# A local attention tile summed by identity products on TensorE, part of the approximate exponentials' additions moved to GpSimd, and the gate products split

## The chip, the cores and the metric

The kernel runs on one core of a Trainium2 chip. The time is the device time of one execution in microseconds (us). The engines are named as in the profile: PE (TensorE matmuls; PEld its weight loads), DVE (VectorE), ACT (ScalarE), POOL (GpSimd), SP (SyncE, which here issues nearly all DMAs). The five run their own instruction streams in order and wait for each other through semaphores.

## The reference

Input x is 2048 rows of 512, bf16. Two attention blocks A and B read the same x, each with its own weights, 32 heads of 16 columns, and their outputs are mixed row by row with a gate:

```python
g = sigmoid((x * gate_w).sum(-1, keepdims=True))
a = A_ref(x, A_wqkv, A_wo)    # full softmax attention: every row sees all 2048 rows
b = B_ref(x, B_wqkv, B_wo)    # local: row s sees rows s, s-2, ..., s-14 (8 of them), masked below row 0
return g * a + (1 - g) * b
```

In B, for one row and head: `logits[w] = q . k[s - 2w] / 4`, a softmax over the 8 values, and `o = sum over w of attn[w] * v[s - 2w]`.

## The kernel before

**Block A** has 32 periods: four blocks of 512 query rows by eight groups of four heads (`periods`). In a period there are 16 tiles of 128 key rows, with four heads each: 64 score blocks of 128 keys by 512 queries, 2048 in all. Each is one matmul of PE with 32 rows of weights; four heads lie in the four row groups of the array and can run side by side. A score block is turned into exponentials in one of two ways:

- Exactly, on ACT: PE writes three or two blocks into one of two PSUM rings (`ring`), ACT reads them with one activation and writes `pT` in bf16 (`act_source`), and PE multiplies `pT` with the values and the ones column of `vp_all` into the period's accumulator `acc` (`emit_pva`).
- Approximately, on DVE, by whole tiles of four blocks, called quads (`make_quad`): PE writes a block into a PSUM bank `m`, DVE multiplies and adds so that the result, written as uint16, is read as the bf16 bit pattern of the exponential (`conv`, four of 128x512). Two further terms are the same numbers plus 42 and plus 85 (`OFFS`); each is one DVE addition over the whole 128x2048 quad (`term`). PE multiplies the three terms with the values and with two weighted copies of them, `vd_all`, and adds them up in `acc` (`emit_pvd`). A quad can only come from the last four key tiles of a period.

At the end of a period DVE transposes `acc`, takes the reciprocal of the sums, POOL scales, and DVE transposes back (`post`). There is one accumulator; the next period's sums wait until it is read.

**Block B** has 16 tiles of 128 rows (`b_tile`). PE projects K, V and Q of the tile, DVE copies them out of PSUM, SP stores K and V into a DRAM scratch `kv_scr` and loads them back eight times, shifted by two rows each (`ksh`, `vsh`, 128 x 8 x 512 bf16). POOL then does nearly everything: eight products q * k, a tree of additions over the 16 columns of a head, the softmax with short steps on DVE and ACT between, eight products of attention and value into f32 tiles (`amul`), seven additions over the eight (`aadd`, `fin1`), the last with a bf16 output `obb`. PE transposes `obb` in 16 small pieces (`fin2`), and DVE copies the result as `obt` (`fin3`). `padd` chains a tile's POOL steps one after the other, but other POOL work can stand between them.

**The gate** is 64 matmuls of one column each (`zmm`), an exponential on ACT and three short DVE operations. **The output** (`final`) multiplies, for each of 16 row tiles, four chunks of `obt` with B's output weights and four of A's result with A's into one PSUM bank; DVE multiplies with the gate, SP stores. For the last four tiles all parts but one of A's are done early and kept in f32; the last part, and the addition, follow the last period.

**The order of the work** is written by a planner inside the kernel (`Sched`), which runs when the program is built. It holds a list of operations with estimated durations, dependencies, buffers (`Hold`, `Slots`) and due times, and takes, over and over, the operation that can begin soonest on its engine, among near ones the one that is due first. The engines' instruction streams come out in that order. What bears on the change:

- `MARGIN` adds a pause to a dependency between two engines, so that an operation is placed only so long after its input's estimated end.
- `warm` and `zero_pass` put matmuls of zeros (`zw` with `ones_t`) into PE's stream. The planner adds up what PE streamed in the last 3413 ns (`share`; a matmul on a quarter of the array counts a quarter). Under `STREAM` a zero matmul may go in where it delays nothing much; under `LEAST` it goes in even with a small delay.
- `lock=True` marks DVE operations that the planner keeps from overlapping with a POOL operation.
- `start_quad` starts a quad on DVE whenever DVE is estimated to be done with it before ACT would have reached that tile, and no other PE work is overdue. So the number of blocks that DVE takes over follows from the planner's estimates of all engines.
- `hooks` runs when a period begins and adds the projections, the gate (period 0) and the B tiles that then come due.
- The loads at the start are issued by SP in the order of their due times, with a time at which the planner expects each to land.

Every instruction passes through one helper (`chain_on`, called at line 382), so that all instructions have line 382 in the profile; they are told apart by the names of their tiles.

Of the kernel before, what the change touches and what calls it, by code (L numbers as in the profile page):

```python
# [10 lines left out]
ALU = mybir.AluOpType  # L11
AX = mybir.AxisListType
FP32 = mybir.dt.float32
BF16 = mybir.dt.bfloat16
# [5 lines left out]
DH = 16  # L20
# [34 lines left out]
PASS = 216.0  # L55
SWITCH = 100.0

MARGIN = {("POOL", "DVE"): 1500.0, ("POOL", "PE"): 1500.0, ("DVE", "PE"): 200.0, ("PE", "DVE"): 60.0,
          ("ACT", "DVE"): 1000.0, ("DVE", "POOL"): 800.0, ("SP", "POOL"): 1500.0, ("POOL", "ACT"): 1000.0}
WINDOW = 3413.0  # L60
STREAM = 0.48
LEAST = 0.42
FAST = 682.0


# [52 lines left out]
class Sched:  # L118
# [31 lines left out]
    def pe_run(self, mms, start, state=None, count=False):  # L150
        t, mode, busy = (self.t["PE"], self.pe_mode, list(self.pe_busy)) if state is None else state
        busy = list(busy)
        t = max(t, start)
        first = None
        last = t
        for m, tile_, cols in mms:
            if m != mode:
                if state is None and count:
                    self.switches += 1
                t = max(t, max(busy) + (SWITCH if "r" in (m, mode) else 0.0))  # L160
                mode = m
            ks = range(4) if tile_ is None else (tile_,)
            t = max(t, max(busy[k] for k in ks))
            if first is None:
                first = t
            if count:
                self.streamed.append((t, t + cols / 2.4, 1.0 if tile_ is None else 0.25))
            for k in ks:
                busy[k] = t + cols / 2.4 + 2.5
            last = t + 174.0 + cols / 2.4  # L170
            t += 15.0
        return first, last, (t, mode, busy)
# [159 lines left out]
def kernel(  # L332
# [138 lines left out]
    def dma(o, i):  # L471
        return lambda: SP.dma_start(out=o, in_=i)
# [34 lines left out]
        ld[(kind, 0)] = S_.add(Op("SP", lambda: None, dur=1.0, due=-9.0, lat=7000.0, name=f"ld_{kind}"))  # L507
    load("x0", x_load(0), 8100.0)
    load("x1", x_load(1), 11500.0)
    load("wv", dma(wv[:, :, G1:D], a_w3[:, :, 2 * D + G1:3 * D]), 9000.0)  # L510

    def gw_load():
        with nc.allow_non_contiguous_dma(reason="tiny gate vector load"):
            SP.dma_start(out=gw[:], in_=gate_w.rearrange("(c p) -> p c", p=128))
    load("gw", gw_load, 9000.0)
    load("bw", dma(bw[:], B_wqkv.rearrange("(c p) n -> p c n", p=128)), 12000.0)

    def pad_load():
        for k in range(2 * D // 128):
            SP.dma_start(out=kv_scr[0:16, 128 * k:128 * k + 128], in_=zw[0:16, :])  # L520
    ld["pad"] = S_.add(Op("SP", pad_load, dur=4500.0, due=2000.0, lat=3000.0, name="ld_pad"))
# [177 lines left out]
    def g_jobs(due):  # L699
        st = {}  # L700
        hz = Hold("m")

        def zmm():
            st["zp"] = misc_ps(hz, [128, NT])
            for t in range(NT):
                for c in range(DC):
                    mm(st["zp"][:, t:t + 1], xT[:, c, t * 128:(t + 1) * 128], gw[:, c:c + 1], c == 0, c == DC - 1)

        def zexp():
            st["e1"] = const.tile([128, NT], FP32, name="e1")  # L710
            A.activation(out=st["e1"][:], in_=st["zp"][:], func=ACT.Exp, scale=-1.0)

        def zfin():
            d1 = const.tile([128, NT], FP32, name="d1")
            V.tensor_scalar_min(out=ratio[:], in0=st["e1"][:], scalar1=1.0e30)
            V.tensor_scalar_add(out=d1[:], in0=ratio[:], scalar1=1.0)
            V.reciprocal(out=gate[:], in_=d1[:])
        ops = [Op("PE", zmm, mms=[("f", None, 70)] * 64, due=due, deps=[o for v in xt_ops.values() for o in v] + [ld["gw"]],
                  acq=[hz], not_before=due - 4000.0, name="z"),
               Op("ACT", zexp, dur=250.0, allow=0.0, rel=[hz], name="zexp"),  # L720
               Op("DVE", zfin, dur=600.0, allow=3000.0, name="zfin")]
        S_.chain(ops)
        g_done.append(ops[-1])
# [14 lines left out]
    def b_tile(t, due):  # L738
# [71 lines left out]
            if t == NT - 1:  # L810
                S_.add(lv)
        pool = []
        hp = [Hold("prod") for _ in range(3)]

        def padd(fn, dur, after_last=True, early=False, **kw):
            late = len(pool) > 17 and not early
# [75 lines left out]
        hobb = Hold("osb")  # L892

        def amul(w_, k):
            def s():
                if w_ == 0:
                    st["prod"] = work.tile([128, WH, D], FP32, name="prod", tag="prod", bufs=1)
# [6 lines left out]
        def aadd(k):  # L904

            def s():
                prod = st["prod"]
                G.tensor_tensor(out=prod[:, k, :], in0=prod[:, k, :], in1=prod[:, k + 1, :], op=ALU.add)
            return s

        def fin1():
            obb = sb(hobb, [128, D], BF16, "obb")
            G.tensor_tensor(out=obb[:], in0=st["prod"][:, 0, :], in1=st["prod"][:, 1, :], op=ALU.add)
            st["obb"] = obb
        level, added = [], False
        for w_ in range(W):
            padd(amul(w_, len(level)), 1094.0, after_last=added or w_ == 0, acq=[hp[2]] if w_ == 0 else [], deps=[lv] if w_ == 0 else [],
                 rel=[hvs, hlg] if w_ == W - 1 else [])
            level.append(0)
            added = False  # L920
            while len(level) > 1 and level[-1] == level[-2] and len(level) + level[-1] < 5 and (level[-1] < 2):
                padd(aadd(len(level) - 2), 1268.0)
                added = True
                level.pop()
                level[-1] += 1
        padd(fin1, 1270.0, acq=[hobb], rel=[hp[2]])
        hb = Hold("m")
        obt_hold[t] = Hold("keep")

        def fin2():  # L930
            st["ptp"] = misc_ps(hb, [128, DC, 128], BF16)
            for c in range(DC):
                for c4 in range(4):
# [7 lines left out]
        f = [Op("PE", fin2, mms=[("c", j, 128) for _ in range(DC) for j in range(4)], allow=4000.0, acq=[hb, obt_hold[t]], rel=[hobb],  # L941
                deps=[pool[-1]], name="bf2"),
             Op("DVE", fin3, dur=415.0, allow=800.0, rel=[hb], name="bf3")]
        S_.chain(f)
        obt_ops[t] = f[-1]

# [363 lines left out]
    LATE = 2000.0  # L1310
    QUAD = 6000.0
    UNIT = 470.0
    quad_at = [0]
    quad_end = [None]

# [37 lines left out]
    def make_quad(p, t, late):  # L1353
        i = periods[p][1]
        hq = [Hold("dt") for _ in OFFS]
        q = dict(p=p, t=t, hold=hq, terms=[], late=late)

        def term_tile():
            q["terms"].append(sb(hq[len(q["terms"])], [128, 4, QW], U16, "dt"))
        aops, fops = [], []  # L1360
        for j in range(4):
            hold = Hold("m")
# [9 lines left out]

            def conv(j=j, st=st):
                if j == 0:
                    term_tile()
                V.tensor_scalar(out=q["terms"][0][:, j, :], in0=st["s"][:], scalar1=EXP_MULT, scalar2=EXP_ADD,
                                op0=ALU.mult, op1=ALU.add)
            f_ = S_.add(Op("PE", fill, mms=[("r", j, 512)], deps=[qt_ops[periods[p]][0], kdep(p, t)],
# [5 lines left out]
                           name="conv"))  # L1384
            aops.append(a_)
        tops = []
        for k in range(1, len(OFFS)):
            def term(k=k):
                term_tile()
                V.tensor_scalar(out=q["terms"][k][:], in0=q["terms"][0][:], scalar1=float(OFFS[k]), scalar2=None, op0=ALU.add)  # L1390
            tops.append(S_.add(Op("DVE", term, dur=FAST, lock=True, deps=aops + tops[-1:], acq=[hq[k]], due=min(S_.now + 7000.0 + 1500.0 * k, late - 4000.0 + 1000.0 * k), name="term")))

        def done(o):
            d_busy[0] -= 1
            q["vis"] = o.vis
            pvd_ready.append(q)
        tops[-1].after = done
        d_busy[0] += 1

    def d_source(e):  # L1400
# [31 lines left out]
    def hooks(p):  # L1432
# [90 lines left out]
```

## Time and profile before

| | us |
|---|---|
| median of 3 runs | 819.74 (811.35 to 826.09) |
| the profiled execution | 810.39 |
| its span, first to last instruction | 808.5 |
| ACT busy | 753.4 |
| PE busy | 734.4 |
| POOL busy | 705.7 |
| DVE busy | 691.1 |
| score exponentials on ACT, 650 | 745.2 |
| DVE conversions (128x512), 424 | 277.2 |
| DVE additions (128x2048), 212 | 235.6 |
| mean granted PE clock | 0.971 |

The profile page gives for each engine the busy time, its share of the span and the number of instructions, then the span in 40 slices with tenths of busy time (the row PEclk is the clock granted to PE, in tenths of full speed), then the chain of work that ended last, followed back from the last instruction. Groups of instructions carry tile names, output first: `dt<-m_ps` is a DVE conversion of a score block, `dt<-dt` a DVE addition for a further term, `prod<-vsh,lg` a POOL product of values and attention. A group's busy time counts overlapping instructions once, so it can be less than count times mean. Busy times of PE are of pipelined matmuls with modelled ends; a PE that is 91% busy is not at its peak. A line of the waits reads: engine and tile that waited, what it waited for, us in total, times, longest.

### The profile page before, as it was taken

What the parts mean: (1) busy time and instruction counts of PE and PEld (TensorE: products, weight loads), DVE (VectorE), ACT (ScalarE), POOL (GpSimd) and SP (SyncE); (2) the same over time, 40 slices, a digit from 0 to 9 for tenths busy, and PEclk for the clock granted to TensorE, in tenths of its full rate; (3) what the DMA queues carried; (4) which work ended last, traced back from release to release, by engine and by line L of the source; (5) the groups of instructions that cost most, each with busy time, mean ns of one, the idle gap of its engine ahead of it and who ended that gap; (6) DMA issues with size and microseconds to landing.
All of it is one profiled execution on the core that took longest, in us unless ns stands there. A gap on an engine that the chain in (4) does not pass through costs nothing.

```text
span 808.5 us, 19646 instructions
## 1 busy us (share of the span) xinstructions
PE 734.4 (91%) x8132; PEld 232.4 (29%) x8183; DVE 691.1 (85%) x1019; ACT 753.4 (93%) x680; POOL 705.7 (87%) x615
## 2 busy tenths in 40 slices
PE   7989989899989898999999989999989999999896
PEld 2332222232322213222332222233222222223222
DVE  3635889989999898999999899999988998888974
ACT  3998889998999979998999999999999999999993
POOL 1289798999999979897998999999897999999995
PEclk9997999999999979998999999999989999999998
DMA  8470210220115211011215211111013110212101
GB/s 202 141 117 1 67 53 28 91 67 30 42 50 78 68 53 60 20 54 53 67 51 42 67 53 66 54 49 60 26 53 92 53 54 17 66 64 67 60 14 34
DMA packets 100937, 48.22 MB, mean 60 GB/s; under 512 B 61936, under 2 KB 98288, under 8 KB 100848
## 3 DMA queue, kind: packets, MB, share of 16 engines
q1 hardware_dynamic: 99264, 46.57, 21.3%
q8 instruction: 64, 1.05, 0.5%
q10 hardware_dynamic: 1584, 0.39, 0.2%
q14 instruction: 25, 0.20, 0.1%
HBM read 38.54 MB, written 6.32 MB: 55 GB/s over the span
## 4 chain that ended last, share of the span: by engine, by line
DVE 32%; PE 28%; ACT 27%; issue 9%; SPq 2%; DMA 1%; ACTq 0%; DVEq 0%
ACT pT L382 27%; DVE dt L382 23%; PE m_ps L382 13%; PE acc L382 8%; PE ring L382 7%; DVE kt_all L382 2%; DVE qt L382 2%; SPq L382 2%; DMA bw<-in_B_wqkv_dram 1%; DVE kmax_all L382 1%; DVE kvs L382 1%; DVE accT L382 1%; DVE qb L382 0%; DVE kadd L382 0%; DVE oat L382 0%
## 5 line engine op out<-in xcount | busy, mean ns | idle before, releaser
L382 ACT ACTIVATE pT<-ring 128x1536 bf16<-128x1536 f32 (+2 forms) x650 | 745.2, 1292 | 29.9 <-PE ring L382 28.1
L382 PE MATMUL ring<-qt,kt_all 32*128 32x512 bf16 x1624 | 280.4, 389 | 30.6 <-ACT pT L382 24.9
L382 DVE TENSOR_SCALAR dt<-m_ps 128x512 uint16<-128x512 f32 x424 | 277.2, 676 | 30.5 <-PE m_ps L382 19.4
L382 POOL TENSOR_TENSOR prod<-prod 128x512 f32<-128x512 f32 x224 | 291.8, 1308 | 10.4
L382 DVE TENSOR_SCALAR dt<-dt 128x2048 uint16<-128x2048 uint16 x212 | 235.6, 1114 | 1.1 <-PE acc L382 0.6
L382 POOL TENSOR_TENSOR prod<-ksh,qb 128x512 f32<-128x512 bf16 x128 | 164.8, 1315 | 37.7 <-DVE kt_all L382 33.0
L382 PEld LDWEIGHTS <-kt_all 32*128 32x128 bf16 (+1 forms) x2304 | 94.2, 92 | 299.8 <-issue 284.4
L382 PE MATMUL m_ps<-qt,kt_all 32*128 32x512 bf16 x424 | 149.5, 390 | 19.7 <-DVE dt L382 13.5
L382 PE MATMUL acc<-pT,vp_all 128*17 128x512 bf16 x1624 | 158.9, 389 | 3.4 <-issue 3.0
L382 POOL TENSOR_TENSOR prod<-vsh,lg 128x512 f32<-128x512 bf16 x128 | 156.1, 1239 | 2.9
L382 PEld LDWEIGHTS <-vp_all 128*17 128x17 bf16 x2048 | 46.1, 88 | 112.0 <-issue 102.7
L382 PE MATMUL acc<-dt,vd_all 128*17 128x512 bf16 x848 | 65.8, 386 | 0.8 <-DVE dt L382 0.8
L382 PE MATMUL m_ps<-bw,xT 128*32 128x512 bf16 x768 | 56.7, 395 | 2.1 <-DVE dt L382 0.8
L382 PE MATMUL acc<-ones_t,zw 128*32 128x512 bf16 (+1 forms) x230 | 50.0, 400 | 3.2 <-DVE accT L382 2.0
L382 PE MATMUL acc<-dt,vp_all 128*17 128x512 bf16 x424 | 42.3, 389 | 0.8 <-issue 0.8
L382 PEld LDWEIGHTS <-xT 128*32 128x32 bf16 (+1 forms) x1152 | 32.3, 97 | 33.7 <-issue 26.5
L382 PE MATMUL m_ps<-xT,wkd 128*32 128x512 bf16 x512 | 39.9, 406 | 2.2 <-DMA xT<-in_A_x_dram 0.9
L382 POOL TENSOR_TENSOR ott<-accT,rden 128x256 bf16<-128x256 f32 x31 | 22.9, 740 | 21.5 <-DVE rden L382 20.0
L382 PE MATMUL m_ps<-xT,wqd 128*32 128x512 bf16 x496 | 35.8, 382 | 0.6 <-DVE kt_all L382 0.3
L382 PEld LDWEIGHTS <-zw 128*128 128x128 bf16 (+1 forms) x285 | 17.3, 95 | 53.1 <-issue 51.3
L382 DVE CAST kvs<-m_ps 128x512 bf16<-128x512 f32 x32 | 21.7, 680 | 12.4 <-PE m_ps L382 12.3
L382 DVE CAST qt<-m_ps 128x512 bf16<-128x512 f32 x31 | 21.1, 680 | 12.1 <-PE m_ps L382 11.9
(69 smaller groups left out, 409.2 us busy)
## 6 DMA issues: line engine op xcount, KB each, us to landing
ksh<-kv_scr SPq DMA_DIRECT2D x16, 1024.0 KB, 5.4
vsh<-kv_scr SPq DMA_DIRECT2D x16, 1024.0 KB, 5.5
kv_scr<-kvs SPq DMA_DIRECT2D x16, 256.0 KB, 2.0
out_dram<-osb SPq DMA_DIRECT2D x16, 128.0 KB, 1.7
bw<-in_B_wqkv_dram SPq DMA_DIRECT2D x1, 1536.0 KB, 9.7
wkd<-in_A_wqkv_dram SPq DMA_DIRECT2D x24, 32.0 KB, 3.7
wqd<-in_A_wqkv_dram SPq DMA_DIRECT2D x24, 32.0 KB, 2.9
bwo<-in_B_wo_dram SPq DMA_DIRECT2D x1, 512.0 KB, 4.3
```

What stands on the lines that cost most here:

```text
L382: return chain_on(key, f(*a, **k))
```

## The change

In `b_tile` the products of attention and value are written over the loaded values, in bf16, and the seven additions and the 16 transposes are replaced by matmuls: for each of four column chunks PE takes the eight product tiles as weights and the identity as the moving operand, and adds them up in PSUM, which sums and transposes at once. The f32 result is copied by DVE.

In `make_quad` every other quad has its first addition (plus 42) done by POOL, in two halves of 128x1024; the second stays on DVE. The quad's matmuls on `acc` wait for both.

The gate's 64 matmuls become four operations of 16, which the planner may place apart and no longer counts as PE activity. Constants of the planner change: two margins are halved, both thresholds for zero matmuls rise by 0.02. The start loads are reordered (B's projection weights first) with later expected landings, eight pad transfers become one, and a B tile is begun 0.8 periods later.

```diff
-MARGIN = {("POOL", "DVE"): 1500.0, ("POOL", "PE"): 1500.0, ("DVE", "PE"): 200.0, ("PE", "DVE"): 60.0,
+MARGIN = {("POOL", "DVE"): 1500.0, ("POOL", "PE"): 1500.0, ("DVE", "PE"): 100.0, ("PE", "DVE"): 30.0,
...
-STREAM = 0.48
-LEAST = 0.42
+STREAM = 0.50
+LEAST = 0.44
...
-            if count:
+            if count and m != "z":
                 self.streamed.append((t, t + cols / 2.4, 1.0 if tile_ is None else 0.25))
...
-    load("wv", dma(wv[:, :, G1:D], a_w3[:, :, 2 * D + G1:3 * D]), 9000.0)
+    load("bw", dma(bw[:], B_wqkv.rearrange("(c p) n -> p c n", p=128)), 20500.0)
...
-    load("gw", gw_load, 9000.0)
-    load("bw", dma(bw[:], B_wqkv.rearrange("(c p) n -> p c n", p=128)), 12000.0)
+    load("gw", gw_load, 22000.0)
+    load("wv", dma(wv[:, :, G1:D], a_w3[:, :, 2 * D + G1:3 * D]), 24000.0)
...
-        def zmm():
-            st["zp"] = misc_ps(hz, [128, NT])
-            for t in range(NT):
-                for c in range(DC):
-                    mm(st["zp"][:, t:t + 1], xT[:, c, t * 128:(t + 1) * 128], gw[:, c:c + 1], c == 0, c == DC - 1)
+        def zmm(b):
+            def s():
+                if b == 0:
+                    st["zp"] = misc_ps(hz, [128, NT])
+                for t in range(4 * b, 4 * b + 4):
+                    for c in range(DC):
+                        mm(st["zp"][:, t:t + 1], xT[:, c, t * 128:(t + 1) * 128], gw[:, c:c + 1], c == 0, c == DC - 1)
+            return s
...
-        ops = [Op("PE", zmm, mms=[("f", None, 70)] * 64, due=due, deps=[o for v in xt_ops.values() for o in v] + [ld["gw"]],
-                  acq=[hz], not_before=due - 4000.0, name="z"),
+        ops = [Op("PE", zmm(b), mms=[("z", None, 70)] * 16, due=due + 300.0 * b, deps=[o for v in xt_ops.values() for o in v] + [ld["gw"]] if b == 0 else [],
+                  acq=[hz] if b == 0 else [], not_before=due - 4000.0 + 1000.0 * b, name="z") for b in range(4)]
...
-                G.tensor_tensor(out=st["prod"][:, k, :].rearrange("p (h d) -> p h d", d=DH),
-                                in0=st["vsh"][:, w_, :].rearrange("p (h d) -> p h d", d=DH), in1=attn_bc, op=ALU.mult)
+                v_ = st["vsh"][:, w_, :].rearrange("p (h d) -> p h d", d=DH)
+                G.tensor_tensor(out=v_, in0=v_, in1=attn_bc, op=ALU.mult)
...
-                G.tensor_tensor(out=prod[:, k, :], in0=prod[:, k, :], in1=prod[:, k + 1, :], op=ALU.add)
...
-            G.tensor_tensor(out=obb[:], in0=st["prod"][:, 0, :], in1=st["prod"][:, 1, :], op=ALU.add)
...
-                    T.transpose(out=st["ptp"][32 * c4:32 * c4 + 32, c, :],
-                                in_=st["obb"][:, c * 128 + 32 * c4:c * 128 + 32 * c4 + 32],
-                                identity=ident[:], tile_position=(0, 32 * c4))
+        def vsum(c):
+            def s():
+                if c == 0:
+                    st["ptp"] = misc_ps(hb, [128, DC, 128])
+                for w_ in range(W):
+                    mm(st["ptp"][:, c, :], st["vsh"][:, w_, c * 128:(c + 1) * 128], ident[:], w_ == 0, w_ == W - 1)
+            return s
...
+    POOLED = 0.5
+    PARTS = 2
...
+        n_terms[0] += POOLED
+        pooled = n_terms[0] >= 1.0
+        if pooled:
+            n_terms[0] -= 1.0
+            def part(a, b):
+                def s():
+                    if a == 0:
+                        term_tile(1)
+                    G.tensor_scalar(out=q["terms"][1][:, a:b, :], in0=q["terms"][0][:, a:b, :], scalar1=float(OFFS[1]), scalar2=None, op0=ALU.add)
+                return s
+            n = PARTS
+            for a in range(0, 4, 4 // n):
+                o = Op("POOL", part(a, a + 4 // n), dur=80.0 + 2050.0 / n, deps=aops[a:a + 4 // n], acq=[hq[1]] if a == 0 else [], due=-0.5, name="pterm")
...
-        while b_next[0] < NT and b_next[0] * 1.7 <= p + 1.8:
+        while b_next[0] < NT and b_next[0] * 1.7 <= p + 1.0:
```

More of the change, by code (lines that the diff above doesn't have):

```diff
@@ L514, in gw_load @@
             SP.dma_start(out=gw[:], in_=gate_w.rearrange("(c p) -> p c", p=128))
-    load("gw", gw_load, 9000.0)
-    load("bw", dma(bw[:], B_wqkv.rearrange("(c p) n -> p c n", p=128)), 12000.0)
+    load("gw", gw_load, 22000.0)
+    load("wv", dma(wv[:, :, G1:D], a_w3[:, :, 2 * D + G1:3 * D]), 24000.0)
     def pad_load():
-        for k in range(2 * D // 128):
-            SP.dma_start(out=kv_scr[0:16, 128 * k:128 * k + 128], in_=zw[0:16, :])
-    ld["pad"] = S_.add(Op("SP", pad_load, dur=4500.0, due=2000.0, lat=3000.0, name="ld_pad"))
+        SP.dma_start(out=kv_scr[0:16, :].rearrange("r (k n) -> r k n", n=128), in_=_ap(zw[0:16, :], [list(zw[0:16, :].ap[0]), [0, 2 * D // 128], [1, 128]]))
+    ld["pad"] = S_.add(Op("SP", pad_load, dur=1500.0, due=2000.0, lat=3000.0, name="ld_pad"))
     ld["bwo"] = S_.add(Op("SP", dma(bwo[:], B_wo.rearrange("(c p) n -> p c n", p=128)), dur=1500.0, due=2100.0, lat=6000.0, name="ld_bwo"))
@@ L717, in zfin @@
             V.reciprocal(out=gate[:], in_=d1[:])
-        ops = [Op("PE", zmm, mms=[("f", None, 70)] * 64, due=due, deps=[o for v in xt_ops.values() for o in v] + [ld["gw"]],
-                  acq=[hz], not_before=due - 4000.0, name="z"),
+        ops = [Op("PE", zmm(b), mms=[("z", None, 70)] * 16, due=due + 300.0 * b, deps=[o for v in xt_ops.values() for o in v] + [ld["gw"]] if b == 0 else [],
+                  acq=[hz] if b == 0 else [], not_before=due - 4000.0 + 1000.0 * b, name="z") for b in range(4)]
+        ops += [
                Op("ACT", zexp, dur=250.0, allow=0.0, rel=[hz], name="zexp"),
@@ L812, in b_tile @@
         pool = []
-        hp = [Hold("prod") for _ in range(3)]
+        hp = [Hold("prod") for _ in range(2)]
         def padd(fn, dur, after_last=True, early=False, **kw):
@@ L891, in b_tile, with amul @@
         padd(sm_norm, 628.0)
-        hobb = Hold("osb")
-        def amul(w_, k):
+        def amul(w_):
             def s():
-                if w_ == 0:
-                    st["prod"] = work.tile([128, WH, D], FP32, name="prod", tag="prod", bufs=1)
                 a0 = st["lg"][:, :, w_:w_ + 1]
                 attn_bc = _ap(a0, [list(a0.ap[0]), [W, H], [0, DH]])
-                G.tensor_tensor(out=st["prod"][:, k, :].rearrange("p (h d) -> p h d", d=DH),
-                                in0=st["vsh"][:, w_, :].rearrange("p (h d) -> p h d", d=DH), in1=attn_bc, op=ALU.mult)
-            return s
@@ L904, in aadd @@
-        def aadd(k):
-            def s():
-                prod = st["prod"]
-                G.tensor_tensor(out=prod[:, k, :], in0=prod[:, k, :], in1=prod[:, k + 1, :], op=ALU.add)
-            return s
-        def fin1():
-            obb = sb(hobb, [128, D], BF16, "obb")
-            G.tensor_tensor(out=obb[:], in0=st["prod"][:, 0, :], in1=st["prod"][:, 1, :], op=ALU.add)
-            st["obb"] = obb
-        level, added = [], False
-        for w_ in range(W):
[L917 to L925, printed above, removed]
@@ L926, in b_tile @@
-        padd(fin1, 1270.0, acq=[hobb], rel=[hp[2]])
+                v_ = st["vsh"][:, w_, :].rearrange("p (h d) -> p h d", d=DH)
+                G.tensor_tensor(out=v_, in0=v_, in1=attn_bc, op=ALU.mult)
+            return s
+        for w_ in range(W):
+            padd(amul(w_), 1094.0, after_last=w_ == 0, deps=[lv] if w_ == 0 else [], rel=[hlg] if w_ == W - 1 else [])
         hb = Hold("m")
         obt_hold[t] = Hold("keep")
[L930 to L933, printed above, removed]
-                    T.transpose(out=st["ptp"][32 * c4:32 * c4 + 32, c, :],
-                                in_=st["obb"][:, c * 128 + 32 * c4:c * 128 + 32 * c4 + 32],
-                                identity=ident[:], tile_position=(0, 32 * c4))
+        def vsum(c):
[5 more added lines that the diff above has]
+            return s
@@ L940, in fin3 @@
             V.tensor_copy(out=obt_tiles[t], in_=st["ptp"][:])
-        f = [Op("PE", fin2, mms=[("c", j, 128) for _ in range(DC) for j in range(4)], allow=4000.0, acq=[hb, obt_hold[t]], rel=[hobb],
-                deps=[pool[-1]], name="bf2"),
-             Op("DVE", fin3, dur=415.0, allow=800.0, rel=[hb], name="bf3")]
+        f = [Op("PE", vsum(c), mms=[("f", None, 140)] * W, allow=4000.0 if c == 0 else -3000.0, acq=[hb, obt_hold[t]] if c == 0 else [],
+                rel=[hvs] if c == DC - 1 else [], deps=[pool[-1]] if c == 0 else [], name="bf2") for c in range(DC)]
+        f.append(Op("DVE", fin3, dur=683.0, allow=800.0, rel=[hb], name="bf3"))
         S_.chain(f)
@@ L1312 @@
     UNIT = 470.0
+    POOLED = 0.5
+    PARTS = 2
+    n_terms = [0.0]
     quad_at = [0]
@@ L1355, in make_quad, with term_tile @@
         hq = [Hold("dt") for _ in OFFS]
-        q = dict(p=p, t=t, hold=hq, terms=[], late=late)
-        def term_tile():
-            q["terms"].append(sb(hq[len(q["terms"])], [128, 4, QW], U16, "dt"))
+        q = dict(p=p, t=t, hold=hq, terms=[None] * len(OFFS), late=late)
+        def term_tile(k):
+            q["terms"][k] = sb(hq[k], [128, 4, QW], U16, "dt")
         aops, fops = [], []
@@ L1374, in conv @@
                 if j == 0:
-                    term_tile()
+                    term_tile(0)
                 V.tensor_scalar(out=q["terms"][0][:, j, :], in0=st["s"][:], scalar1=EXP_MULT, scalar2=EXP_ADD,
@@ L1386, in make_quad @@
         tops = []
-        for k in range(1, len(OFFS)):
+        n_terms[0] += POOLED
[11 more added lines that the diff above has]
+                o = Op("POOL", part(a, a + 4 // n), dur=80.0 + 2050.0 / n, deps=aops[a:a + 4 // n], acq=[hq[1]] if a == 0 else [], due=-0.5, name="pterm")
+                o.gap = 30.0
+                tops.append(S_.add(o))
+        for k in range(2 if pooled else 1, len(OFFS)):
             def term(k=k):
-                term_tile()
+                term_tile(k)
                 V.tensor_scalar(out=q["terms"][k][:], in0=q["terms"][0][:], scalar1=float(OFFS[k]), scalar2=None, op0=ALU.add)
-            tops.append(S_.add(Op("DVE", term, dur=FAST, lock=True, deps=aops + tops[-1:], acq=[hq[k]], due=min(S_.now + 7000.0 + 1500.0 * k, late - 4000.0 + 1000.0 * k), name="term")))
+            tops.append(S_.add(Op("DVE", term, dur=FAST, lock=True, deps=aops + (tops[-1:] if not pooled else []), acq=[hq[k]], due=min(S_.now + 7000.0 + 1500.0 * k, late - 4000.0 + 1000.0 * k), name="term")))
         def done(o):
+            if any(x.vis is None for x in tops):
+                return
             d_busy[0] -= 1
-            q["vis"] = o.vis
+            q["vis"] = max(x.vis for x in tops)
             pvd_ready.append(q)
-        tops[-1].after = done
+        for x in tops:
+            x.after = done
         d_busy[0] += 1
```

## The prediction

> **What bounds the kernel now.** I read the engine shares first, then the chain, then the waits, then stretches of time. The first lines of the page:
>
> ```profile
> PE 734.4 (91%) x8132; PEld 232.4 (29%) x8183; DVE 691.1 (85%) x1019; ACT 753.4 (93%) x680; POOL 705.7 (87%) x615
> PEclk9997999999999979998999999999989999999998
> DVE 32%; PE 28%; ACT 27%; issue 9%; SPq 2%; DMA 1%; ACTq 0%; DVEq 0%
> ```
>
> Four engines are over 85% busy, and the chain that ended last is passed among DVE, PE and ACT; POOL is not on it. ACT is fullest: the softmax exponentials run at its rate. Its 808.5 us are 753.4 of work and 55.1 of idle time. Of the idle time 13.6 us lie before 20 us (ACT works 6.44 of the first 20), and 12.4 come after its last exponential at 796.1. About 29 remain in the middle, and the waits name their source:
>
> ```profile
> ACT pT L382 <- PE ring L382: 28.1, 42, 2.2
> PE ring L382 <- ACT pT L382: 25.2, 76, 0.8
> PE m_ps L382 <- DVE dt L382: 15.9, 39, 1.5
> ```
>
> ACT waits 28.1 us for scores from PE, in 42 places; PE waits as often for ACT to free a score buffer. The clock row shows dips, so I asked for the stretches around those I found:
>
> ```profile
> 69.20:84.00 14.80, 14.26 (x83) 2.73 (x86) 9.51 (x16) 11.17 (x10) 14.33 (x17) 0.54 0.00 1
> 117.00:122.00 5.00, 5.00 (x45) 1.12 (x42) 3.08 (x5) 2.59 (x4) 4.69 (x6) 0.66 0.00 0
> 287.70:300.00 12.30, 12.30 (x89) 2.36 (x85) 10.88 (x13) 8.86 (x8) 11.83 (x10) 0.59 0.27 87
> 373.00:382.00 9.00, 8.98 (x80) 1.98 (x76) 7.15 (x10) 6.12 (x6) 5.82 (x6) 0.62 0.04 13
> 601.70:611.00 9.30, 8.36 (x74) 2.28 (x72) 7.36 (x11) 6.69 (x6) 8.99 (x9) 0.64 0.00 0
> ```
>
> Columns: stretch, length, busy us of PE, PEld, DVE, ACT, POOL, then the granted clock. In these five stretches (50.4 us) the clock is near half and ACT is idle for 3.6 + 2.4 + 3.4 + 2.9 + 2.6 = 15.0 us. So half of ACT's waiting comes from a slowed PE and 14 us from everything else. The timeline shows what precedes the first dip:
>
> ```profile
> 65.25 1.75 PE L382 MATMUL m_ps<-gw,xT 128*128 128x1 bf16 x64
> ```
>
> These 64 gate matmuls stream one column each, yet the planner books them as 70 columns of PE activity. Ahead of the dips at 117 and 287.7 us stand PE waits for a DVE conversion (1.13 us at 116.83; 0.52, 0.48, 0.24 and 0.26 us from 283.87).
>
> **The change part by part**, against the profiled execution (810.39 us, span 808.5; 1.9 us lie around it).
>
> *Exponentials.* The order of the changed program has 322 + 323 score exponentials on ACT for 325 + 324 + 1 before: 1612 score blocks of 512 columns for 1624. Three blocks take 1505 ns and two 1081, so a block costs 424 ns: 12 x 0.424 = 5.1 us. The union of the 650 is 745.2 us, of which 1624 x 0.424 = 688.6 is blocks, so 0.087 us is the fixed part of one; five fewer save 0.4. **-5.5 us**, on the path.
>
> *DVE.* The 12 blocks come to it as 12 conversions (x 0.676 = +8.1 us); its additions on 128x2048 fall from 212 to 164 (48 x 1.114 = -53.5); the copies of the local result read f32 sums (16 x (0.68 - 0.417) = +4.2). About -41 us: 650 busy. DVE stands on the chain because its conversions free the banks into which PE writes, so its relief shows in the 15.9 us above. I credit it only below, against PE.
>
> *POOL.* Out go 96 additions (x 1.398) and 16 final ones (22.9 us): -157 us. The products keep their count, and now write bf16 over their input (1.24 us each now, taken as equal). In come 108 additions of 128x1024 uint16, which the trace does not have. Lower end: the memsets, 128x1 at 0.10 us and 128x128 at 0.20, 0.82 ns an element, 0.94 us for 1024. Upper end: two-input rows, medians 0.43 us for 128 elements and 1.268 for 512, 2.18 ns an element, 2.39 us. An operation with one input lies between; the nearest one-input row, the affine select (0.40 us at 128, 0.63 at 256), gives 1.99. I take 1.55, the middle of the memset and two-input slopes (1.5 ns x 1024): +167 us. POOL comes to 715 us against 706. Cover: POOL is on no link of the chain; if the new additions are late they are, because PE waits for them, and that is the slow rival.
>
> The Trainium skill (GPSIMD Engine Reference, Engine selection) advises against POOL for elementwise work but calls one-input operations roughly line-rate. At its 1.2 GHz that is an estimate of 0.85 us for 1024 elements, with the 0.10 of the shortest memset 0.95, and POOL at 652 us; no run here shows it yet.
>
> ```profile
> L382 DVE TENSOR_SCALAR dt<-dt x212: 620/1076/1792, 77.9 to 791.3; 128x2048 uint16<-128x2048 uint16 x106
> L382 POOL TENSOR_TENSOR prod<-vsh,lg x128: 1089/1100/1602, 81.1 to 794.5; 128x512 f32<-128x512 bf16 x128
> ```
>
> Shortest, median, longest: the DVE addition alone takes 0.62 us, mostly far more, and POOL operations too are stretched at times, by about 0.5 us. The two engines exclude each other. The Trainium skill (SBUF — State Buffer, Who interferes with whom) says so: one port pair is locked for a whole instruction and the loser fully blocks. That speaks against putting the additions on POOL: each blocks another of the 164 left on DVE. By the rule the stretch per DVE addition (1.114 - 0.62 = 0.49 us) stays as long as POOL stays as busy, which I have assumed by keeping 1.114.
>
> *PE.* In come 32 products with the identity per tile, 512 in all, 128x128 on 128 columns. The nearest row is the V projection of the same shape: 192 take 14.7 us, 0.077 each, +39 us. Out go 256 small transposes (-6.9 us). Zero matmuls on the accumulator fall from 153 to 100: 0.21 us each where three stand in a row (0.81 us against 0.39 for one), -11 us. Moving three quads: 0.078 x 24 + 0.1 x 12 + 0.353 x 12 for the approximate path, -(0.098 + 0.173) x 12 for the exact one: +4. Together **+25 us** of PE, 759 of some 800: its idle time falls from 74 to about 50 us. Lower bound of the cost: nothing, since the zero matmuls stood in time that PE had to spare. Upper bound: ACT's 14 us of waits outside the dips grow as the slack shrinks, by 74/50: +7. DVE's relief works against it. I take the middle, **+3.5**.
>
> *Clock.* The gate matmuls are split in four parts of 16 and no longer counted as activity, and both thresholds for zero matmuls rise by 0.02. The first dip should go: **-3.6 us**. The other 11.4 us I credit at nothing: the planner's pause between DVE's result and PE's use is halved (200 to 100 ns), and exactly such waits precede two of the dips. Below nothing: one more dip costs 2.4 to 3.6. The Trainium skill (TensorE: Matmul & The Clock Gate, Part 1) says the gate measures activity over windows of about 3.4 us; the first dip, 13.65 us long, is four of these. It also says (Part 4) that transposes do not count as activity, which would favour the new products.
>
> *Head and tail.* The load of B's projection is moved ahead of two others on SP; PE waits 0.84 us for it now, and the first exponential (19.82 us) depends on x alone: nothing. Eight small pad transfers (9.45 us of SP's queue) become one; SP issues nothing urgent behind them except the 512 KB output weights: nothing. Local tiles start 0.8 periods later, while POOL's end today is that of the last local tile:
>
> ```profile
> L382 POOL TENSOR_TENSOR obb<-prod x16: 1262/1334/1727, 106.9 to 798.3; 128x512 bf16<-128x512 f32 x16
> 801.45 2.73 PE m_ps L382 x24
> 805.05 0.75 DVE osb L382
> ```
>
> The last local sum ends at 799.7 us, 3.6 after ACT; its transposes, projection and a gate product then stand between the output tiles. In the changed order the local work ends ahead of the last four output tiles, which follow each other on DVE: from the first at 799.99, 4 x 0.75 = 802.99 instead of 805.80: **-2.8 us**.
>
> Sum: 810.4 - 5.5 + 3.5 - 3.6 - 2.8 = **802.0**, 1.0% under its own profile. The runs of before reach from 811.35 to 826.09 with a median of 819.74, 1.2% over the profiled one; scaled up, 811.2. A kernel with one dip fewer should have less of this spread, so I forecast **805 us**, 1.8% under the median.
>
> **Rivals.**
> 1. *The clock holds (0.30).* More full-array work, higher thresholds, a lighter DVE. For it: 15 of 29 us of waits lie in five dips; against it: the halved pauses. Four more dips gone: 802.0 - 11.4 = 790.6, -2.4% on the profile.
> 2. *POOL becomes the bound (0.13; slower).* An accumulation on PE now waits for an addition that is queued on POOL, in order, behind products of 1.1 to 1.3 us, and everything on PE behind it (scores for ACT too) waits along. POOL has about 760 us between its first product at 36.3 and the end of ACT; without the new additions it needs 549. So it decides from (760 - 549)/108 = 1.95 us an addition. At the two-input price of 2.39 POOL needs 549 + 258 = 807, 47 over: about 849 us.
> 3. *A balanced trade (0.17).* The waits for POOL, or more dips, eat the gains: 5.5 + 2.8 saved, 7 more on PE, an extra dip at 3.6: 812 on the profile, 815 to 822 in the runs.
>
> My forecast has the remaining 0.40.
>
> **How the numbers follow.** A change under 2% can hardly be told from none with this spread. Range: down to 789 (rival 1), up to 824 (rival 3 in a poor run); beyond lie rival 2 and extremes. Faster by over 2%: rival 1 with a fifth of the forecast, 0.38. Within 2%: 0.48. Slower: 0.14.
>
> **What would show it.** The new POOL row at or under 1.6 us; POOL absent from PE's waits; no dip around the gate matmuls; about 760 us of PE; ACT's score work near 740 us; four output tiles in a row at the end. I am wrong if PE waits for POOL for more than 10 us in total, or if the clock has more than five dips.

## The result, and the profile after

| | before | after |
|---|---|---|
| median us | 822.91 (4 runs, 811.35 to 827.27) | 925.93 (4 runs, 920.3 to 930.62) |
| profiled execution | 810.39 | 924.93 |
| ratio after to before | | 1.137, 95% interval 1.130 to 1.143 |

The kernel became 13.7% slower; I had forecast 805 us. Ratios leave out disturbed runs, so they need not be those of the medians. The head of the changed kernel's page, with the clock and the chain:

```profile
span 922.9 us, 20033 instructions
PE 804.4 (87%) x8371; PEld 256.1 (28%) x8408; DVE 654.0 (71%) x983; ACT 755.9 (82%) x675; POOL 831.7 (90%) x611
PEclk9979795998987989698899799778898897799998
POOL 71%; PE 12%; ACT 6%; DVE 5%; issue 4%; SPq 1%; DMA 1%; DVEq 0%; ACTq 0%; POOLq 0%
```

POOL, which was on no link of the chain before, makes up 71% of it. DVE (654.0 us) and ACT (755.9) are busy for about as long as before, and idle in the time that was added. Three rows of POOL's instructions (count, then busy us and mean ns of one, then idle time before them) say why:

```profile
L382 POOL TENSOR_SCALAR dt<-dt 128x1024 uint16<-128x1024 uint16 x108 | 314.4, 2914 | 23.8 <-DVE dt L382 23.7
L382 POOL TENSOR_TENSOR prod<-ksh,qb 128x512 f32<-128x512 bf16 x128 | 155.7, 1238 | 33.0 <-DMA ksh<-kv_scr 32.1
L382 POOL TENSOR_TENSOR vsh<-vsh,lg 128x512 bf16<-128x512 bf16 x128 | 150.7, 1197 | 0.1
```

One new addition of 128x1024 takes 2.914 us on average (shortest 2.757, median 2.770), where I took 1.55 with a ceiling of 2.39, and where the planner's code books 80 + 2050/2 = 1105 ns. The waits of the changed kernel:

```profile
ACT pT L382 <- PE ring L382: 110.6, 100, 6.6
DVE dt L382 <- PE m_ps L382: 71.4, 79, 6.9
ACT lg L382 <- POOL lg L382: 27.3, 9, 11.0
PE acc L382 <- POOL dt L382: 23.2, 11, 3.5
```

Only 23.2 us are booked on PE as waits for POOL, but ACT's wait for scores grew from 28.1 to 110.6 us. ACT also waits 27.3 us for POOL itself, for the logits (`lg`) of local tiles, which are queued among the additions; before, the waits show none of this kind. How a wait of PE for POOL becomes one of ACT for scores is seen in the timeline: POOL, then PE, then ACT around 137 us, in one order of time:

```profile
131.88 5.93 POOL L382 TENSOR_SCALAR dt<-dt 128x1024 uint16<-128x1024 uint16 x2
...
137.87 0.60 PE L382 MATMUL acc<-dt,vd_all 128*17 128x512 bf16 x6 [1.86 <-POOL dt L382]
...
138.41 0.60 PE L382 MATMUL ring<-qt,kt_all 32*128 32x512 bf16 x2
...
139.10 2.37 ACT L382 ACTIVATE pT<-ring 128x1024 bf16<-128x1024 f32 x2 [2.06 <-PE ring L382]
```

Two additions end at 137.8; PE stands 1.86 us before a product that reads them; the score matmuls behind it come late, and ACT is idle for 2.06 us. Then the clock falls. The stretch right behind (length, busy us of PE, PEld, DVE, ACT, POOL, clock, then the DMA's busy share and GB/s):

```profile
140.00:154.00 14.00, 14.00 (x96) 4.67 (x95) 7.98 (x11) 9.91 (x9) 14.00 (x10) 0.50 0.24 77
```

PE runs at half its clock, and ACT is idle for 4.1 of 14 us. The clock row above shows such dips all along the span; the mean is 0.888 for 0.971. So a lateness seems to be paid twice, as a stop and as a slow stretch behind it. That the stop brings the slow stretch on is read from the order in time; what supports it is that the same order of instructions with a cheaper addition has only three dips before the end (below).

### The profile page after: what moved, and what is told of

Same layout as the page of the kernel before. It is cut to its first block, busy times and chain, and to the rows that moved or that the text cites. A ratio compares the mean times of both kernels' runs of the same rounds, so it can differ in the third digit from the quotient of the medians.

```text
span 922.9 us, 20033 instructions
## 1 busy us (share of the span) xinstructions
PE 804.4 (87%) x8371; PEld 256.1 (28%) x8408; DVE 654.0 (71%) x983; ACT 755.9 (82%) x675; POOL 831.7 (90%) x611
## 4 chain that ended last, share of the span: by engine, by line
POOL 71%; PE 12%; ACT 6%; DVE 5%; issue 4%; SPq 1%; DMA 1%; DVEq 0%; ACTq 0%; POOLq 0%
POOL prod L382 27%; POOL dt L382 27%; POOL vsh L382 11%; ACT pT L382 6%; PE m_ps L382 6%; DVE dt L382 3%; POOL lg L382 3%; PE acc L382 3%; PE ring L382 2%; POOL ott L382 2%; SPq L382 1%; POOL rr L382 0%; DMA xT<-in_A_x_dram 0%; DVE kt_all L382 0%; DVE kmax_all L382 0%
## 5 line engine op out<-in xcount | busy, mean ns | idle before, releaser
L382 ACT ACTIVATE pT<-ring 128x1536 bf16<-128x1536 f32 (+1 forms) x645 | 745.0, 1275 | 114.8 <-PE ring L382 110.6
L382 DVE TENSOR_SCALAR dt<-m_ps 128x512 uint16<-128x512 f32 x436 | 289.4, 680 | 114.0 <-PE m_ps L382 71.4
L382 POOL TENSOR_SCALAR dt<-dt 128x1024 uint16<-128x1024 uint16 x108 | 314.4, 2914 | 23.8 <-DVE dt L382 23.7
L382 PE MATMUL ring<-qt,kt_all 32*128 32x512 bf16 x1612 | 301.2, 416 | 31.4 <-ACT pT L382 27.7
L382 PE MATMUL m_ps<-qt,kt_all 32*128 32x512 bf16 x436 | 163.9, 420 | 23.2 <-DVE dt L382 12.2
L382 DVE TENSOR_SCALAR dt<-dt 128x2048 uint16<-128x2048 uint16 x164 | 177.5, 1087 | 3.3 <-PE acc L382 1.9
L382 POOL TENSOR_TENSOR prod<-prod 128x512 f32<-128x512 f32 (+1 forms) x128 | 152.5, 1200 | 1.3
L382 POOL TENSOR_TENSOR vsh<-vsh,lg 128x512 bf16<-128x512 bf16 x128 | 150.7, 1197 | 0.1
L382 PE MATMUL acc<-dt,vd_all 128*17 128x512 bf16 x872 | 76.7, 413 | 28.2 <-POOL dt L382 23.2
L382 PE MATMUL m_ps<-ident,vsh 128*128 128x128 bf16 x512 | 39.4, 225 | 0.1
L382 DVE CAST kt_all<-m_ps 128x512 bf16<-128x512 f32 x36 | 24.7, 685 | 18.0 <-PE m_ps L382 17.7
```

Source lines behind the costliest of these rows:

```text
L382: return chain_on(key, f(*a, **k))
```

## The experiments

All ratios are to the kernel before, run on the same chip.

### The additions taken off POOL

```diff
-    POOLED = 0.5
+    POOLED = 0.0
```

> The changed kernel with all additions of the quads on DVE (108 POOL additions become 54 additions of 128x2048 on DVE); the exponentials on ACT stay 322 + 323. Price theory (the uint16 addition on POOL at 2.77 us made POOL the bound, and nothing else costs): 800 to 812 us, POOL near 550 us busy, ACT's wait for scores near 30 us, five or fewer clock dips. Order theory (halved margins, the 512 identity products and the new thresholds make PE late by themselves): above 870 us, the dips stay.

Measured: 810.02 us, ratio 0.995 (0.990 to 0.9999); POOL 545.0 us busy, ACT's wait for scores 31.0 us, six clock dips ahead of the end. The price theory holds, but for one dip more than it allowed. All else in the change together is worth about half a per cent here; the interval reaches from nothing to the 1% that I had summed. The gate's dip, from which 3.6 us of that sum were to come, did not go (below).

### The same queues, a cheaper addition

Two neighbouring uint16 are added as one int32. The terms are bit patterns of positive bf16 numbers, so adding 42 never carries out of the lower half. Every engine's order stays as in the changed kernel.

```diff
-                    G.tensor_scalar(out=q["terms"][1][:, a:b, :], in0=q["terms"][0][:, a:b, :], scalar1=float(OFFS[1]), scalar2=None, op0=ALU.add)
+                    o_ = q["terms"][1][:, a:b, :].rearrange("p j n -> p (j n)").bitcast(I32)
+                    i_ = q["terms"][0][:, a:b, :].rearrange("p j n -> p (j n)").bitcast(I32)
+                    c_ = off32[:].bitcast(I32)      # a 128x2 uint16 tile of 42
+                    G.tensor_tensor(out=o_, in0=i_, in1=_ap(c_, [list(c_.ap[0]), [0, (b - a) * QW // 2]]), op=ALU.add)
```

> The changed kernel, every engine's order unchanged; each POOL addition takes two neighbouring uint16 as one int32 and adds a constant tile holding 85 or 42 in both halves (42 here), 512 elements with two inputs instead of 1024 with one. Price theory: one takes 1.1 to 1.4 us (the two-input rows of 512 elements), POOL comes to 690 us and the kernel to 800 to 815 us. Order theory, and the theory that POOL's additions hurt by blocking DVE's: the queues and the number of POOL instructions are the same, so 880 us or more. If an int32 addition is as slow as the uint16 one (2.7 us), nothing moves: 925.

Measured: 788.75 us, ratio 0.972 (0.968 to 0.977). It beats both kernels; its median lies 137 us under that of the change as it was given, and below the 800 to 815 us that I expected. From the head of its page:

```profile
PE 745.8 (94%) x8408; PEld 255.3 (32%) x8408; DVE 642.0 (81%) x984; ACT 744.7 (94%) x675; POOL 651.9 (82%) x611
PEclk9989999999999999999999999998999999999998
...
ACT 42%; PE 36%; issue 11%; DVE 8%; SPq 1%; DMA 1%; ACTq 0%; DVEq 0%
```

The tile's own view has its POOL addition (shortest, median, longest ns):

```profile
L382 POOL TENSOR_TENSOR dt<-dt,off x108: 1032/1042/1545, 44.2 to 765.5; 128x512 int32<-128x512 int32 x108
```

It has the same number of POOL instructions at 1.04 us instead of 2.77. POOL is off the chain, the dips are down to three before the end, the granted clock is 0.984 to 0.993 over its runs (0.959 to 0.977 without POOL additions). Since the order of every queue is that of the slow kernel, neither the order, nor the margins, nor the number of POOL's instructions made the change slow by itself; the price of one did. POOL's blocking of DVE is a small part at most: DVE's 164 additions take 167.7 us here and 177.5 in the slow kernel.

### The planner told the price

```diff
-                o = Op("POOL", part(a, a + 4 // n), dur=80.0 + 2050.0 / n, ...
+                o = Op("POOL", part(a, a + 4 // n), dur=80.0 + 5380.0 / n, ...
```

(The second half also waits for the first to be placed.)

> The changed kernel, with the planner's duration of the POOL addition raised from 1.105 to 2.77 us (the measured one); it then places 412 conversions and 102 POOL additions and plans for a late POOL. Throughput theory: POOL needs 549 + 102 x 2.9 = 845 us plus some 36 before its first product, so 880 us or more whatever the plan. Surprise theory (the loss is that PE's order does not know how late POOL is, so PE stands still and its clock falls): 820 to 850, with far fewer dips and PE's waits for POOL near nothing.

Measured: 898.88 us, ratio 1.107 (1.100 to 1.114). Throughput wins over surprise. The stretches of this run (columns as above):

```profile
40.00:775.00 735.00, 690.68 (x7551) 229.67 (x7554) 584.20 (x875) 712.75 (x638) 696.78 (x488) 0.99 0.17 46
775.00:895.20 120.20, 51.51 (x487) 25.34 (x479) 20.43 (x34) 15.83 (x18) 104.13 (x108) 0.69 0.22 68
```

With a true price in the plan the additions come in time and the clock stays at 0.99 until 775 us, but then POOL still has 104 us of local tiles to do, nearly alone. The same overload appears as a long tail here and as stops all along in the changed kernel; a plan that knows the price gains 27 us (898.88 against 925.93), of 137 that the packed form gains.

### The additions alone

The kernel before with only the POOL additions (106 halves) in `make_quad`; in a second one they have the packed form.

> The kernel before with only the POOL additions (106 of them), everything else as before. Price theory: POOL needs 706 + 106 x 2.9 = 1013 us plus 36 at the start, so about 1050 us, with POOL over 93% busy. A theory in which the local sum by PE is what makes POOL's additions costly: 925 or less.

Measured: 1032.12 us, ratio 1.271 (1.264 to 1.279); POOL 965.9 us busy (94%). This is near the 1050 of the price theory.

> The kernel before with POOL additions in packed int32 form and nothing else of the change. POOL needs 706 + 106 x 1.1 = 823 us and 36 at the start. Throughput theory: the cheap addition alone has no room, about 860 to 875 us, POOL over 93% busy; the local sum on PE is what makes the room. If POOL's additions pay for themselves by what DVE is spared: 800 to 830.

Measured: 880.09 us, ratio 1.082 (1.068 to 1.095). Even at the low price POOL has no room beside the old local sum, and again ends alone:

```profile
40.00:790.00 750.00, 683.92 (x7578) 218.15 (x7623) 607.29 (x919) 720.97 (x646) 710.90 (x638) 0.98 0.19 50
790.00:878.90 88.90, 12.45 (x144) 4.33 (x144) 8.17 (x15) 0.83 (x2) 77.14 (x74) 0.54 0.12 40
```

So the two parts belong together: the local sum on PE makes the room, the additions use it, and they fit at 1.04 us and not at 2.77; no price between was run. POOL's share was 90% busy here, not over 93% as I expected.

### What is slow about the addition

Six forms in turn, in the order of the changed kernel. The three products do not give the sum that belongs there; they are run for their price alone.

```diff
+                    f_ = form[0] % 6
+                    form[0] += 1
+                    # 0: two tensor_scalar adds of 512 uint16; 1: tensor_scalar mult, 1024 bf16
+                    # 2: tensor_tensor mult, 1024 bf16;        3: tensor_scalar mult, 512 f32
+                    # 4: tensor_scalar add, 1024 uint16;       5: tensor_tensor add, 512 int32
```

> The changed kernel, order unchanged; the 108 half additions on POOL take six forms in turn, to price each on the same data: uint16 plus scalar as two of 512, uint16 plus scalar of 1024, bf16 times scalar of 1024, bf16 times tensor of 1024, f32 times scalar of 512, int32 plus tensor of 512. The three products stand in for the addition there, so those terms are only approximated. Type theory (16-bit integers are what is slow): uint16 near 2.7 ns an element, bf16 times scalar near 1.0 to 1.5 ns (1.0 to 1.5 us), int32 1.04 us as before. Scalar theory (any operation with a scalar is slow on POOL): bf16 and f32 times scalar also near 2.7 ns an element (2.8 and 1.4 us), the tensor forms 2.0 to 2.3 us for 1024.

Measured (one run): the rows of the additions and their stand-ins (count, then busy us and mean ns).

```profile
L382 POOL TENSOR_SCALAR dt<-dt 128x512 uint16<-128x512 uint16 x36 | 57.7, 1617 | 0.5 <-DVE dt L382 0.5
L382 POOL TENSOR_SCALAR dt<-dt 128x1024 uint16<-128x1024 uint16 x18 | 53.5, 2971 | 17.7 <-DVE dt L382 17.7
L382 POOL TENSOR_SCALAR dt<-dt 128x1024 bf16<-128x1024 bf16 x18 | 52.2, 2902 | 1.3 <-DVE dt L382 1.3
L382 POOL TENSOR_TENSOR dt<-dt,ones_t 128x1024 bf16<-128x1024 bf16 x18 | 35.6, 1979 | 7.6 <-DVE dt L382 7.6
L382 POOL TENSOR_SCALAR dt<-dt 128x512 f32<-128x512 f32 x18 | 29.4, 1634 | 0.4 <-DVE dt L382 0.4
L382 POOL TENSOR_TENSOR dt<-dt,off 128x512 int32<-128x512 int32 x18 | 20.7, 1151 | 1.6 <-DVE dt L382 1.6
```

The scalar theory holds, the type theory falls. With a scalar, 1024 elements take 2.90 us in bf16 and 2.97 in uint16, and 512 take 1.62 in uint16 and 1.63 in f32; for uint16 that is (2971 - 1617)/512 = 2.6 ns an element. With a second tensor in place of the scalar (one column, read again and again), 1024 bf16 take 1.98 us. The packed form wins twice: it halves the elements and has no scalar. An addition of unpacked uint16 with a second tensor was not run, and why a scalar costs more stays open.

### The rest of the change, split

The kernel before with only the local sum on PE; and the changed kernel without it and without POOL additions, which leaves the planner's constants, the loads, the split gate and the later local tiles.

> The kernel before with only the local sum on PE (products in place, identity products, f32 copy). The planner then gives ACT 16 blocks more (1640). POOL 549 us, PE 39 us of identity products more. If POOL's release is worth something by itself (fewer locked DVE additions): 800 to 808, ratio 0.985 to 0.995. If the local sum only moves work to PE: 810 to 822, ratio 1.00 to 1.01.

Measured: ratio 0.988 (0.978 to 0.998), in the range of the first theory; that locked DVE additions are the reason was not tested.

> The changed kernel without POOL additions and without the local sum on PE: planner constants, loads, split gate products, later local tiles. ACT gets the same 1612 blocks as with the whole change. If the 5.5 us of ACT work and the tail are worth what I put on them: 802 to 808, ratio 0.985 to 0.995. If the halved margins give it back as waits of PE and dips: 812 to 825, ratio 1.00 to 1.02. Prediction's step on the gate: no clock dip around the gate products.

Measured: ratio 1.007 (1.002 to 1.012). The local sum is worth about 1% alone; the other edits together, which were not separated, cost about 0.7% where POOL and DVE are loaded as before, though ACT has the 12 blocks fewer that I credited with 5.5 us. Both kernels are planned afresh, so each ratio is that of an edit with the order that it brings.

### The packed kernel, varied

One edit each on the packed kernel: three quarters of the quads on POOL; the gate products in one operation, booked as before; margins of 200 and 60 again; thresholds of 0.48 and 0.42 again.

> The packed int32 addition with three of four quads' first additions on POOL (166 halves) instead of two of four; ACT 1604 blocks. POOL about 549 + 166 x 1.1 = 730 us. If DVE still holds PE back: 782 to 788 us. If POOL's queue is what additions wait for: 790 to 800.

Measured: 797.37 us, ratio 0.981 (0.973 to 0.990), POOL 704.3 us busy. The interval overlaps that of half the quads (0.968 to 0.977), so the two are not told apart; nothing speaks for more than half.

> The packed int32 kernel with the gate's 64 products in one operation again, booked as PE activity as before. In the packed kernel with the split gate ACT stood idle 5.8 us in the dip from 52 to 64 us. If the split causes or lengthens that dip: 784 to 787 us, a dip of 13.7 us at most. If the split helps as the prediction had it (3.6 us): 791 to 794. If the dip has nothing to do with the gate: 788 to 790.

Measured: 793.04 us, ratio 0.975 (0.965 to 0.985): not told apart from 0.972. The products now stand in one piece at 107 us instead of in parts from 52 us on, and its profile has no dip near either place; the time doesn't show a gain from that.

> The packed int32 kernel with the two margins at 200 and 60 ns again; ACT gets 8 blocks more (+3.4 us). If the halved margins cost more in PE's waits than they win: 780 to 787 us. If they are what lets the planner move blocks to DVE: 791 to 796.

Measured: 795.02 us, ratio 0.978 (0.969 to 0.987): the intervals overlap, so this decides nothing about the halved margins.

> The packed int32 kernel with the zero-matmul thresholds at 0.48 and 0.42 again; ACT gets 4 blocks fewer (-1.7 us), zero matmuls on the accumulator fall from 100 to 81. If the raised thresholds keep the clock up: more dips than three, 791 to 800 us. If they do nothing: 786 to 789.

Measured: 811.9 us, ratio 0.999 (0.995 to 1.003). The granted clock is 0.958 to 0.981 over its ten runs, against 0.984 to 0.993 with the raised thresholds. So nearly all that the packed kernel wins is lost with 0.02 of threshold, or with the other order that this brings: the two were not separated.

## Why the prediction was wrong

**POOL: the step that failed.** "An operation with one input lies between" the memset and the two-input rows. It lies above both: 2.77 against my upper end of 2.39. I took the number of inputs for the measure of the cost. The one row of the right kind, a POOL operation with a scalar, was in the trace before, `rr` with 128x32 (shortest, median and longest ns):

```profile
L382 POOL TENSOR_SCALAR rr<-rr,ratio x16: 353/362/892, 70.0 to 768.0; 128x32 f32<-128x32 f32 x16
```

One size gives no slope, but a median of 0.36 us for 32 elements beside 0.43 for 128 of a two-input row was a sign that it is not the cheaper kind. With the fixed part and slope of the six forms, 0.26 + 32 x 0.0026 = 0.34 us, the row fits the high price. And my nearest one-input row, the affine select, gave 1.99 us, above the 1.95 from which I had POOL as the bound; I took 1.55 instead. That POOL stood on no link of the chain was no cover: at 2.77 it became the chain. The sign that I had named for being wrong came too: PE waits 23.2 us for POOL, where I allowed 10.

**Rival 2 had the mechanism and the point.** It said that from 1.95 us an addition POOL is the bound, because PE's accumulations wait for a queue that is full. At 2.914 its formula gives 549 + 108 x 2.914 - 760 = 104 us over, so 802 + 104 = 906; the run has 924.93. The 19 us left are not accounted for: POOL waits for DVE in its turn (23.7 us), but its busy time, 831.7 us, is also less than the 864 of the formula. I gave it 0.13, because I held its ceiling to be the two-input price; yet of my own range for the price, 0.94 to 2.39, three tenths lie above 1.95.

**ACT's blocks and the planner.** I asked the program's order how many blocks ACT keeps and took its 12 fewer as a gain. But the planner hands out blocks by its own durations, here 1105 ns for an operation of 2770. The order told truly what is issued, not whether it fits. In the packed kernel, where the duration is nearly true, the score exponentials take 736.2 us for 745.2 before: -9.0, where I said -5.5. In the changed kernel itself they take 745.0, and none of it was saved.

**PE** was nearly right. The 512 identity products take 39.4 us of busy time (predicted 39; in the packed kernel 38.0). In the packed kernel PE is 745.8 us busy, not 759, and ACT's wait for scores falls to 18.4 us: the added PE work cost nothing that shows.

**The gate's dip** did not go: the changed kernel has one of 10.2 us from about 51 us on, the packed one of the same length, the one without POOL additions 17.1 us:

```profile
52.00:70.00 18.00, 18.00 (x206) 7.67 (x202) 11.69 (x20) 10.29 (x10) 8.94 (x8) 0.53 0.00 1
```

Here ACT is idle for 7.7 of 18 us, twice what the first dip cost before (3.6). Not booking the products as activity did not hold the clock here; in one piece, and later, in the packed kernel, there was no dip beside them. But the split does not bring the dip by itself either: with three quarters of the quads on POOL the split products stand from 51.2 to 55.6 us, and the clock is 1.00 from 45 to 66 us. What decides it stays open, and the gain of this step was not there.

**The tail** was right. From the last transpose of the accumulator to the end of the last output tile it was 796.52 to 805.80, 9.3 us; in the packed kernel 782.11 to 788.43, 6.3 us, and in the changed kernel 6.2. Predicted -2.8, measured -3.0 in the packed kernel.

**The clock's other dips** I credited at nothing. The packed kernel has two dips besides the gate's, where the kernel before has four besides the first, and its profiled 792.84 us is near my rival 1 (790.6). But rival 1 stood for an addition of 1.55 us, and the packed one takes 1.04; and with the old thresholds the gain is gone (811.9 us). What the change would have done at 1.55 was not run.

**The advice against POOL.** The Trainium skill (GPSIMD Engine Reference, Engine selection) calls one-input elementwise operations on POOL roughly line-rate, from which I estimated 0.95 us for 1024 elements; the runs show 2.76 to 2.97, and the measurement decides. Its advice in the same row, to keep elementwise work off POOL, was the better guide.

## What to carry to other kernels

An operation that the trace doesn't show is priced by a row of its own kind, however small, and not by rows that look simpler: on POOL a scalar operand made an operation dearer than a second tensor. When a planner decides the order, its program shows what it intends at its own prices; check the price of each new operation before reading a gain from the counts. When work is moved to an engine that is off the path, compute the price at which it becomes the path, and give the chance of reaching it the share of your price range that lies beyond that point.

## What was not expected of the hardware

- POOL operations with a scalar took nearly the same time for equal counts of uint16, bf16 and f32: 2.90 to 2.97 us for 1024 elements and 1.62 to 1.63 for 512, against 1.9 us for 1024 bf16 with a second tensor (median 1.894) and 1.04 us for 512 int32, at which size f32 additions before took 1.27.
- A DVE addition, which excludes POOL, can be kept waiting not by one POOL operation but by a row of them. In the changed kernel the longest took 8.68 us (the shortest 0.629; the longest before 1.792):

```profile
594.22 8.68 DVE L382 TENSOR_SCALAR dt<-dt 128x2048 uint16<-128x2048 uint16 x1
...
592.28 3.21 POOL L382 TENSOR_TENSOR vsh<-vsh,lg 128x512 bf16<-128x512 bf16 x3
595.45 4.49 POOL L382 TENSOR_TENSOR prod<-ksh,qb 128x512 f32<-128x512 bf16 x4
599.89 2.46 POOL L382 TENSOR_TENSOR prod<-prod 128x512 f32<-128x512 f32 x2
```

  Its lines are DVE's and then POOL's: POOL went through some eight operations, one after the other, with DVE waiting. The Trainium skill (SBUF — State Buffer, Who interferes with whom) has the loser block for a whole instruction; here it was several. The median addition takes 1.030 us, 0.40 over the shortest; why it was so different here stays open.
- The granted clock tracks the time of this kernel closely: among the runs of the packed kernel with the old thresholds 0.962 goes with 814.65 us and 0.981 with 803.64.
